# Layer two's second product as seven products of sums, its gates kept on the chip

## The chip, the cores and the metric

One core of a Trainium2 chip. The metric is the device time of one execution in microseconds, the median of several runs. The engines are TensorE (PE, matmuls, with its weight loads as PEld), VectorE (DVE), ScalarE (ACT), GpSimd (POOL, hardly used here) and SyncE (SP), whose queue issues nearly all transfers.

## The reference

An attention over small windows makes 3072 tokens of 512 numbers. Two layers follow, each a product to 2048 hidden numbers, a gate, and a product back to 512. All is float32.

```
x = attn_out.transpose(0, 2, 1, 3).reshape(3072, 512)
h = x @ w_in1;  g = s * relu(h)**2 + b;            x = g @ w_out1
h = x @ w_in2;  g = h * 1 / (1 + exp(-1.702 * h)); x = g @ w_out2
```

## The kernel before

**Precision.** A matmul operand is held as two pieces, a high part `h` and the rest `l`, and a product is three matmuls: high x high, high x rest, rest x high. "A split" is what makes the pieces: a cast (ACT, sometimes DVE) and a subtraction (DVE).

**Blocks.** The tokens form six blocks of 512. Attention and layer one of blocks 0 to 3 run first (`step`, one unit per block and hidden tile of 128, `j` from 0 to 15; the very first units are 256 tokens wide). Then four stages run, `SEVEN`: layer one of blocks 4 and 5 (stage 0), and layer two of blocks 0 and 1, 2 and 3, 4 and 5 (stages 1 to 3). A stage takes a pair of blocks, `bp` and `bq`, and is one call of `seven(s)`.

**First product of a stage.** Tokens, hidden numbers and the 512 inner numbers are each cut in halves, and the four quarter results are had from seven products of sums instead of eight (Winograd's form of Strassen's scheme). The sums of the weights (`S1` to `S4`) are made once and lie in memory (`wc`); the sums of the tokens (`T1` to `T4`) are made at the stage's start, out of the second layer's input `y1`. One step `p` (8 in a stage, two hidden tiles each) runs the products A, B, A2, C, D, C2, D2, six matmuls of 512 columns each, into the accumulators `ph` (A and C) and `pb` (B and D). Between them ACT copies A's first half (`p1`, L1081) and DVE makes five additions (L1083 to L1101) into four buffers `ys`, each 128 x 512. A2 waits for `p1`, C2 for the addition `u3`, D2 for the addition `c22` (L1094).

**Gates.** Each step gives four gates: two for `bp` (`gh`, `gl`) and two for `bq` (`gq`). In layer two a gate is a sigmoid (ACT, L997), a multiplication (DVE, L1006), a cast (ACT, L1019) and a subtraction (DVE, L1022). Those of `bp` are used in the next step. Those of `bq` go to memory (`gd`, L1041) and come back later (L1136, tiles `gh`, `gl` or `back`), apart from the last two.

**Second product.** `out_of` multiplies one gate by a tile of `w_out`: 12 matmuls of 512 columns (4 slices, 3 terms, L1059) into `accA` and `accB`. The 16 of `bp` run between the products of the steps, the 16 of `bq` after them as a second group. `w_out2` is prepared by `outer(j)`, stored in `wod`, and read back into the 16 tiles `wo` before stage 1 (`reload`); the tiles stay for all three stages.

**Order.** Every instruction group is an `op` with a due mark, durations, dependencies and buffers. A planner (`Plan.order`) plays all of them once and fixes each engine's order; at run time an engine works through its list and waits where its next instruction must. Buffers are counted by tag: `wi` (12 pairs of weight tiles, streamed in stages), `wz` (4), `u` (4), `st` (3), `h` (2, for `ph`), `a`, `accA`, `accB` and `ys` (1 each).

## Time and profile before

| | us |
|---|---|
| median of 3 runs (lowest, highest) | 1108.02 (1105.91, 1109.97) |
| the profiled execution's span | 1110.2 |
| PE busy in it | 1088.7 |
| DVE busy | 711.0 |
| ACT busy | 494.2 |
| attention and layer one of blocks 0 to 3 | to about 448 |
| stage 0 (layer one, blocks 4 and 5) | about 448 to 615 |
| stages 1, 2, 3 (layer two) | about 615 to 779, 779 to 943, 943 to 1106 |

A matmul's record lasts longer than its turn on the engine, since matmuls overlap; the distance of two starts is its price. The column PEclk is the granted clock of TensorE, 1.00 being full speed. "Idle" of an engine names what ended the wait.

### The profile page before, as it was taken

The page shows a single profiled execution, that of the slowest core. Times are in us where ns is not written, and L with a number is a line of the kernel's source. Part 1 is how long each engine was busy: PE and PEld are TensorE (multiplying, and loading weights), DVE is VectorE, ACT ScalarE, POOL GpSimd, SP SyncE. Part 2 cuts the span into 40 slices and gives each one's busy share as a digit, 9 for nine tenths or more (in the row PEclk, how much of TensorE's full clock was granted, in tenths as well). Part 3 has the DMA queues.
Part 4 walks back from the last instruction along what each step waited for, and adds up shares of the span by engine and source line. Part 5 has one row for each costly group of instructions (what it writes and reads, how often), then busy time and mean ns, then how long its engine had stood idle before and what let it go on. Part 6 is the DMA issues. An engine that isn't in the chain of part 4 may idle for free.

```text
span 1110.2 us, 20092 instructions
## 1 busy us (share of the span) xinstructions
PE 1088.7 (98%) x7852; PEld 897.8 (81%) x7852; DVE 711.0 (64%) x1241; ACT 494.2 (45%) x842; POOL 0.7 (0%) x6
## 2 busy tenths in 40 slices
PE   8879999999999999999999999999999999999998
PEld 7768887888878788888888888888888888888886
DVE  6888988878778688687881455660555760655610
ACT  4678865555445455566640433330433430333310
POOL 0000000000000000000000000000000000000000
PEclk9999999999999999999999999999999999999999
DMA  8776627756678783888999965574755574654154
GB/s 326 245 258 209 208 105 248 259 193 219 208 275 267 265 301 117 312 294 279 318 323 382 322 203 200 183 260 144 246 188 201 202 246 155 203 190 142 76 191 150
DMA packets 119406, 252.99 MB, mean 228 GB/s; under 512 B 12816, under 2 KB 29200, under 8 KB 119312
## 3 DMA queue, kind: packets, MB, share of 16 engines
q1 hardware_dynamic: 119024, 251.19, 66.1%
q8 instruction: 62, 1.02, 0.4%
q10 hardware_dynamic: 288, 0.52, 0.1%
q14 instruction: 32, 0.26, 0.1%
HBM read 169.87 MB, written 81.79 MB: 227 GB/s over the span
## 4 chain that ended last, share of the span: by engine, by line
PE 92%; DMA 3%; DVE 2%; issue 1%; ACT 1%; SPq 0%; ACTq 0%; DVEq 0%
PE accA L1059 16%; PE accB L1059 16%; PE accA L640 7%; PE accB L640 7%; PE ph L981 5%; PE ph L983 5%; PE ph L982 5%; PE ph L602 5%; PE ph L603 5%; PE ph L604 5%; PE pb L983 4%; PE pb L981 4%; PE pb L982 4%; DMA st<-w_in 2%; PE o L479 1%; PE sc L418 1%
## 5 line engine op out<-in xcount | busy, mean ns | idle before, releaser
L997 ACT ACTIVATE r<-ys 128x512 f32<-128x512 f32 x72 | 45.5, 632 | 107.6 <-DVE ys L1094 81.2
L1083 DVE TENSOR_TENSOR ys<-pb,ys 128x512 f32<-128x512 f32 x32 | 22.0, 686 | 91.6 <-DMA out<-y 58.7
L602 PE MATMUL ph<-xh,wih 128*128 128x512 f32 (+1 forms) x200 | 79.3, 396 | 0.6 <-DVE xh L223 0.6
L603 PE MATMUL ph<-xl,wih 128*128 128x512 f32 (+1 forms) x200 | 76.6, 383 | 0.7 <-DVE xl L510 0.7
L604 PE MATMUL ph<-xh,wil 128*128 128x512 f32 (+1 forms) x200 | 76.4, 382 | 0.0
L223 ACT COPY y<-accA 128x512 f32<-128x512 f32 x20 | 10.9, 590 | 138.5 <-issue 84.4
L609 ACT ACTIVATE r<-ph 128x512 f32<-128x512 f32 (+1 forms) x66 | 38.5, 584 | 60.4 <-PE ph L604 54.2
L624 ACT CAST gh<-r 128x512 fp32r<-128x512 f32 (+1 forms) x66 | 40.2, 609 | 47.8 <-PE accB L640 31.2
L1094 DVE TENSOR_TENSOR ys<-pb,ys 128x512 f32<-128x512 f32 x32 | 22.1, 691 | 53.9 <-PE pb L983 53.3
L1006 DVE TENSOR_TENSOR r<-ph,r 128x512 f32<-128x512 f32 x24 | 16.6, 691 | 62.2 <-ACT r L997 62.2
L1059 PE MATMUL accA<-woh,gh 128*128 128x512 f32 x138 | 54.0, 391 | 0.0
L1059 PE MATMUL accA<-woh,gl 128*128 128x512 f32 x138 | 53.9, 390 | 0.0
L1059 PE MATMUL accB<-woh,gh 128*128 128x512 f32 x138 | 53.7, 389 | 0.0
L1059 PE MATMUL accA<-wol,gh 128*128 128x512 f32 x138 | 53.7, 389 | 0.0
L1059 PE MATMUL accB<-woh,gl 128*128 128x512 f32 x138 | 53.7, 389 | 0.0
L1059 PE MATMUL accB<-wol,gh 128*128 128x512 f32 x138 | 53.7, 389 | 0.0
L640 PE MATMUL accA<-gl,woh 128*128 128x512 f32 (+1 forms) x132 | 50.9, 385 | 2.2 <-DVE gl L628 2.2
L1019 ACT CAST gh<-r 128x512 fp32r<-128x512 f32 x64 | 39.8, 622 | 29.1 <-DVE r L1006 21.7
L342 ACT ACTIVATE st<-st 128x512 f32<-128x512 uint32 x64 | 42.8, 676 | 22.4 <-DMA st<-w_out 10.7
L640 PE MATMUL accA<-gh,woh 128*128 128x512 f32 (+1 forms) x132 | 51.4, 389 | 1.3 <-ACT gh L624 1.3
L640 PE MATMUL accB<-gl,woh 128*128 128x512 f32 (+1 forms) x132 | 50.6, 383 | 1.2 <-issue 1.2
L640 PE MATMUL accB<-gh,woh 128*128 128x512 f32 (+1 forms) x132 | 51.0, 387 | 0.0
(210 smaller groups left out, 2973.6 us busy)
## 6 DMA issues: line engine op xcount, KB each, us to landing
gd<-gq SPq DMA_DIRECT2D x56, 512.0 KB, 2.7
wih<-wch SPq DMA_DIRECT2D x96, 256.0 KB, 3.5
wil<-wcl SPq DMA_DIRECT2D x96, 256.0 KB, 3.8
st<-w_in SPq DMA_DIRECT2D x32, 512.0 KB, 5.4
st<-w_out SPq DMA_DIRECT2D x32, 512.0 KB, 5.0
back<-gd SPq DMA_DIRECT2D x56, 256.0 KB, 3.1
k<-k_w SPq DMA_DIRECT2D x24, 512.0 KB, 5.6
v<-v_w SPq DMA_DIRECT2D x24, 512.0 KB, 6.1
```

The source lines that it names most:

```text
L342: nc.scalar.activation(out=lo.bitcast(F32), in_=lo, func=AF.Copy, scale=2.0**-51, bias=2.0)
L602: nc.tensor.matmul(ph, wh, xh, start=(k == 0), stop=False)
L603: nc.tensor.matmul(ph, wh, xl, start=False, stop=False)
L604: nc.tensor.matmul(ph, wl, xh, start=False, stop=(k == KT - 1))
L624: nc.scalar.copy(out=T["g", i][0], in_=T["r", i])
L640: nc.tensor.matmul(o, lt, rh, start=fresh and x == 0, stop=(done and x == 2))
L981: nc.tensor.matmul(ph, wh, xh, start=first and i == 0, stop=False, skip_group_check=True)
L982: nc.tensor.matmul(ph, wh, xl, start=False, stop=False, skip_group_check=True)
L983: nc.tensor.matmul(ph, wl, xh, start=False, stop=i == 1, skip_group_check=True)
L997: nc.scalar.activation(out=T[rk], in_=src(), func=AF.Sigmoid, scale=GATE)
L1019: nc.scalar.copy(out=T[key][0], in_=T[rk])
L1059: nc.tensor.matmul(a, lt, rh, start=n == 0 and x == 0, stop=n == NF - 1 and x == 2)
```

## The change

Stages 1 to 3 run a new function, `wino(s)`; stage 0 still runs `seven(0)`. In `wino`:

- The eight steps of the first product run without the second product between them, in the order A, B, C, A2, D, C2, D2. Steps with odd `p` use `accA` and `accB` (names `pc`, `pd`) in place of `ph` and `pb`.
- The gate is one activation (`Gelu_apprx_sigmoid`), written unsplit into one tile `G` that holds all 32 gates of the stage. It lies where the gates and `w_out` tiles of the earlier stages were. Nothing goes to `gd` and back.
- The second product has the same seven-product form. It runs after the first, product by product in the order 0, 4, 1, 5, 3, 6, 2. Each takes 16 gates' worth of `G` (8 tiles, or sums of them made in place), in four portions of two tiles: a cast and a subtraction on 1024 columns make the pieces, in a ring of three buffer pairs (`oj`, `oj`, `oq`). Each tile then takes 12 matmuls with 256 columns (4 slices of 128 tokens, 3 terms), with the gate's piece as the loaded operand.
- The four quarter results are put together by two pairs of ACT copies and six pairs of DVE additions, and each is stored as it is ready.
- `w_out2` is prepared in pairs (`outer(p)`), with its sums, into `wod`, and every stage streams it through the `wi` tiles. Four pairs are prepared up to stage 0, four not before the end of stage 0's first product. `wi` has 8 tiles in place of 12; four others (`wj`) serve as ring.
- The planner counts an operation that takes two buffers of one tag.

```
-NWI = 12
+NWI = 8
+NWJ = 4
+HELD = 4
...
+    plan.tag("wi", NWI)
+    plan.tag("wj", NWJ)
+    plan.tag("wo", NF)
+    plan.tag("wz", NF - NWI - NWJ)
+    plan.tag("q", 2)
...
+    def outer(p, late=()):
+
+        need = 10.0 * (len(units) + 10) + 1380
+        i0, i1 = [("two", 1, 2 * p + x) for x in range(2)]
+        a, b = [words(i, (1, 1, i[2]), need, late) for i in (i0, i1)]
...
+        def sums(e):
+            fresh(1)
+            fresh(2)
+            v0, v1 = u(i0), u(i1)
+            for x, y, z in ((raw(2)[:, hi], v0[:, hi], v0[:, lo]), (raw(1)[:, hi], v1[:, hi], v0[:, hi]),
+                            (raw(1)[:, lo], v1[:, hi], raw(2)[:, hi]), (raw(2)[:, lo], v1[:, lo], raw(1)[:, lo])):
+                nc.vector.tensor_tensor(out=x, in0=y, in1=z, op=ALU.subtract)
...
+        ku, kv = ("u", i0), ("u", i1)
+        done = parts_of(0, lambda: u(i1), 512, [b], [kv], slice(1, 3), True)
+        d = op(need, {"dve": 1.7}, sums, after=[a, b], alloc=[("st", ("qo", p, 1)), ("st", ("qo", p, 2))], uses=[ku, kv])
+        done += parts_of(1, lambda: raw(1), 512, [d], [], slice(3, 5), False)
+        done += parts_of(2, lambda: raw(2), 512, [d], [], slice(5, 7), False)
+        done += parts_of(3, lambda: u(i0)[:, lo], 256, [a], [ku], slice(0, 1), True)
+        o_wod[p] = done
...
+    def wino(s):
+        m, bp, bq = SEVEN[s]
+        base = 10.0 * (len(units) + 10) + 1000 * s
+        slot, holds, ready = operands(s)
+        o_in = {(p, n): stream(s, p, n, base + 40 * p - 0.5) for p in range(NF // 2) for n in range(4)}
...
+        def g_of(ty, z):
+            if not g_tile:
+                g_tile.append(pools["gg"].tile([P, 4, HALF, 512], F32, tag="G", name="G"))
+            return g_tile[0][:, ty, z]
...
+        def space(c, p):
+            if p % 2:
+                return ("accA" if c in "AC" else "accB", ("two", s, p, c in "AC"), "ABCD".index(c) // 2)
+            return ("h", ("h", s, p, c), None) if c in "AC" else ("a", ("two", s, p, False), "BD".index(c))
...
+        def gates(src, ty, p, need, d, uses):
+            def first(e):
+                nc.scalar.activation(out=g_of(ty, p), in_=src(), func=AF.Gelu_apprx_sigmoid if m else AF.Relu)
+
+            def square(e):
+                nc.scalar.activation(out=g_of(ty, p), in_=g_of(ty, p), func=AF.Square)
+
+            def affine(e):
+                nc.vector.tensor_scalar(out=g_of(ty, p), in0=g_of(ty, p), scalar1=sb[:, 0:1], scalar2=sb[:, 1:2], op0=ALU.mult, op1=ALU.add)
+
+            a = b = op(need, {"act": 0.62}, first, after=d + o_gp + free_g.get((ty, p // 2), []), uses=uses)
+            if not m:
+                b = op(need, {"act": 0.62}, square, after=[b])
+                b = op(need, {"dve": 0.54}, affine, after=[b])
+            o_g[ty, p] = b
+            return a
...
+            A = product(p, "A", "A11", "B11", at, [], True)
+            p1 = op(at + 4, {"act": 0.6}, lambda e, p=p, one=one: nc.scalar.copy(out=spot(one), in_=bank("A", p)),
+                    after=[A] + s_one.get(one, []), alloc=[("ys", tmp)] if p == 0 else [], uses=[tmp, space("A", p)[1]])
+            B_ = product(p, "B", "S2", "T2", at + 5, [], True)
+            u2 = add(one, "B", one, at + 9, [B_, p1])
+            C = product(p, "C", "S3", "T3", at + 10, [], True)
+            u3 = add(1, "C", one, at + 14, [C, u2] + s_22)
+            A2 = product(p, "A", "A12", "B21", at + 15, [A, p1], False)
+            D = product(p, "D", "S1", "T1", at + 20, [], True)
+            c22 = add(1, "D", 1, at + 24, [D, u3])
+            C2 = product(p, "C", "A22", "T4", at + 25, [C, u3], False)
+            c21 = add(2, "C", one, at + 29, [C2, u2] + s_21)
+            D2 = product(p, "D", "S4", "B22", at + 30, [D, c22], False)
+            c12 = add(one, "D", one, at + 34, [D2, c21, u3])
...
+            gates(lambda p=p: bank("A", p), 0, p, at + 60, [A2], [space("A", p)[1]])
...
+        at = base + 400
+        pairs_ = [slice(2 * x, 2 * x + 2) for x in range(HALF // 2)]
+        o_s3 = [op(at, {"dve": 1.22}, lambda e, z=z: nc.vector.tensor_tensor(
+            out=g_of(2, z), in0=g_of(0, z), in1=g_of(2, z), op=ALU.subtract),
+            after=[o_g[ty, 2 * x + i] for ty in (0, 2) for i in range(2)]) for x, z in enumerate(pairs_)]
...
+        SOURCE = {0: 0, 4: 2, 1: 1, 5: 3, 3: 2, 6: 0, 2: 1}
+        BANKS = {0: ("a", 0), 4: ("accA", 0), 1: ("accB", 0), 5: ("accA", 0), 3: ("a", 1), 6: ("accB", 1), 2: ("accA", 1)}
...
+            tag = "wj" if rung[0] % 3 else "q"
+            rung[0] += 1
...
+            def high(e):
+                for k in (kh, kl):
+                    T[k] = wp.tile([P, 2, 512], F32R, tag="wj", name="oj", bufs=NWJ) if tag == "wj" else pools["gg"].tile(
+                        [P, 2, 512], F32R, tag="q", name="oq", bufs=2)
+                nc.scalar.copy(out=T[kh], in_=g_of(ty, z))
+
+            def left(e):
+                nc.vector.tensor_tensor(out=T[kl], in0=g_of(ty, z), in1=T[kh].bitcast(F32), op=ALU.subtract)
+
+            h = op(need, {"act": 1.05}, high, after=o_raw[ty, x], alloc=[(tag, kh), (tag, kl)], uses=[kh])
+            l = op(need, {"dve": 1.22}, left, after=[h], uses=[kh, kl])
...
+                gh, gl = [T[key + (v,)][:, p % 2] for v in "hl"]
+                wh, wl = [w[:, p % 2 * 256:p % 2 * 256 + 256] for w in T["wp", s, n, p // 2]]
+                if m:
+                    for t in range(4):
+                        z = slice(t * P, t * P + P)
+                        a = acc[:, t // 2, t % 2 * 256:t % 2 * 256 + 256]
+                        for x, (lt, rh) in enumerate(((gh, wh), (gh, wl), (gl, wh))):
+                            nc.tensor.matmul(a, lt[:, z], rh, start=first and t % 2 == 0 and x == 0,
+                                             stop=p == HALF - 1 and x == 2, skip_group_check=True)
...
+        for i, n in enumerate((0, 4, 1, 5, 3, 6, 2)):
+            here = at + 70 * i
+            wait = [got["y7", b] for b in range(2)] if n == 5 else []
+            prev = []
+            for x in range(HALF // 2):
+                if n == 3:
+                    sums(x, 2, 3, 2, ALU.subtract, here + 16 * x, o_part[4, x])
+                elif n == 6:
+                    sums(x, 0, 0, 2, ALU.add, here + 16 * x, o_part[0, x])
+                elif n == 2:
+                    sums(x, 1, 1, 2, ALU.subtract, here + 16 * x, o_part[1, x])
+                key = split(n, x, here + 16 * x)
+                d = weights_of(n, x, here + 16 * x - 0.5)
+                for p in (2 * x, 2 * x + 1):
+                    prev = [outer_product(n, p, here + 8 * p, key, d, prev + wait)]
...
+                elif n == 3:
+                    got["u2", b] = evac(n, b, b, b, e, [got["y1", b], got["c11", b]])
+                    got["c21", b] = away(5, b, b, e, [got["u2", b]], True, True)
+                elif n == 6:
+                    got["u4", b] = evac(n, b, b, b, e, [got["u2", b], got["c21", b]])
+                    away(None, b, b, e, [got["u4", b], got["y7", b]], False, True)
+                elif n == 2:
+                    away(n, b, b, e, [got["u4", b]], False, False)
...
-        outer(2 * p)
-        outer(2 * p + 1)
-    for s in range(len(SEVEN)):
-        if s == 1:
-            for j in range(NF):
-                reload(j)
-        seven(s)
+    for p in range(HELD):
+        outer(p)
+    one = len(plan.ops)
+    seven(0)
+    two = len(plan.ops)
+    for p in range(HELD, NF // 2):
+        outer(p, step_end)
+    step_ops.extend(range(one, two))
+    o_gp = [op(-1, {"none": 0.0}, follow("gp", "gg", bufs=1), after=step_ops)]
+    for s in range(1, len(SEVEN)):
+        wino(s)
```

**Place 1: PE, the second product, before in stage 2, after at its start in stage 1.** Names: `woh`, `wol`, `wih`, `wil` are pieces of `w_out2`; `gh`, `gl`, `oq`, `oj` pieces of gates. Before:

```order
L1059 MATMUL accA_8126<-woh_7120,gh_8323 128x512
L1059 MATMUL accA_8126<-wol_7121,gh_8323 128x512
L1059 MATMUL accA_8126<-woh_7120,gl_8324 128x512
...
L1059 MATMUL accB_8143<-woh_7120,gh_8323 128x512
L1059 MATMUL accB_8143<-wol_7121,gh_8323 128x512
L1059 MATMUL accB_8143<-woh_7120,gl_8324 128x512
```

After:

```order
L1358 MATMUL pb_7786<-wih_7672,oq_7240 128x256 [waits DMAHW7_49,PE_49]
L1358 MATMUL pb_7786<-wil_7673,oq_7240 128x256 [waits DMAHW0_49]
L1358 MATMUL pb_7786<-wih_7672,oq_7241 128x256
...
L1358 MATMUL pb_7786<-wih_7691,oj_7416 128x256 [waits DMAHW1_49]
L1358 MATMUL pb_7786<-wil_7692,oj_7416 128x256 [waits DMAHW2_49]
L1358 MATMUL pb_7786<-wih_7691,oj_7417 128x256
```

Twelve wide matmuls a tile, into two accumulators, became twelve of half the width into one, with new pieces of weights and gates every 24.

**Place 2: DVE, a step of the first product at the start of stage 2.** `ys<-pb` and `ys<-ph` are the additions, in the order u2, u3, c22, c21, c12. Before, with the multiplications and subtractions of the gates (`r`, `gl`, `gq`) between:

```order
L1083 TENSOR_TENSOR ys<-pb,ys 128x512 [waits PE_49]
L1022 TENSOR_TENSOR gq<-r,gq 128x512 [waits Activation_49]
L1006 TENSOR_TENSOR r<-ph,r 128x512 [waits Activation_49]
L1087 TENSOR_TENSOR ys<-ph,ys 128x512 [waits DVE_49,PE_49]
L1022 TENSOR_TENSOR gl<-r,gh 128x512 [waits Activation_49]
L1094 TENSOR_TENSOR ys<-pb,ys 128x512 [waits DVE_49,PE_49]
L1097 TENSOR_TENSOR ys<-ph,ys 128x512 [waits PE_49]
L1006 TENSOR_TENSOR r<-ys,r 128x512 [waits DMAHW7_49,Activation_49]
L1101 TENSOR_TENSOR ys<-pb,ys 128x512 [waits DVE_49,PE_49]
```

After, an odd step (`pc`, `pd`) and the start of the next:

```order
L1273 TENSOR_TENSOR ys<-pd,ys 128x512 [waits PE_49,Activation_49]
L1273 TENSOR_TENSOR ys<-pc,ys 128x512 [waits DVE_49,PE_49]
L1273 TENSOR_TENSOR ys<-pd,ys 128x512 [waits DVE_49,PE_49]
L1332 TENSOR_TENSOR oq<-G,oq 128x1024 [waits Activation_49]
L1273 TENSOR_TENSOR ys<-pc,ys 128x512 [waits PE_49]
L1273 TENSOR_TENSOR ys<-pd,ys 128x512 [waits DVE_49,PE_49]
L1297 TENSOR_TENSOR G<-G 128x1024 [waits Activation_49]
L1273 TENSOR_TENSOR ys<-pb,ys 128x512 [waits PE_49,Activation_49]
```

After, in stage 1's second step, where the preparation of `w_out2` (`u`, `st`) is still going on:

```order
L1273 TENSOR_TENSOR ys<-pc,ys 128x512 [waits DVE_49,PE_49,Activation_49]
L358 TENSOR_SCALAR u<-u 128x512 [waits DVE_49]
L362 ISA u<-st,u 128x1024 [waits DVE_49,Activation_49] x2
L366 SCALAR_TENSOR_TENSOR u<-st,u 128x512 [waits DVE_49]
L1273 TENSOR_TENSOR ys<-pd,ys 128x512 [waits PE_49]
```

The gates' four operations are gone; in stage 2 one split (`oq<-G`) and one first sum (`G<-G`) stand behind the third and the fifth addition, in stage 1 four operations of the preparation between the second and the third.

**Place 3: DVE, the turn from the fifth to the sixth product of the second product, stage 1.** Before, in the second group, only the next stage's operands stand on DVE, ahead of that stage's first addition:

```order
L899 TENSOR_TENSOR xf<-xf,u 128x512
L223 CAST wzh<-xf 128x512 [waits DVE_49]
L914 TENSOR_TENSOR wzl<-xf,wzh 128x512 [waits DVE_49]
L914 TENSOR_TENSOR wzl<-xf,wzh 128x512 [waits Activation_49]
L1083 TENSOR_TENSOR ys<-pb,ys 128x512 [waits DMAHW3_49,DMAHW4_49,DMAHW0_49,DMAHW7_49,PE_49,Activation_49]
```

After:

```order
L1332 TENSOR_TENSOR oq<-G,oq 128x1024 [waits PE_49,Activation_49]
L1374 TENSOR_TENSOR ys<-pb,ys 128x512 [waits PE_49]
L1374 TENSOR_TENSOR ys<-pb,ys 128x512
L1384 TENSOR_TENSOR y<-pc,ys 128x512 [waits DVE_49]
L1384 TENSOR_TENSOR y<-pc,ys 128x512 [waits DMAHW7_49,DVE_49]
L1332 TENSOR_TENSOR oj<-G,oj 128x1024 [waits Activation_49]
```

Four additions out of the accumulators of the product that has just ended now stand between two splits; 22 of the stage's 28 splits are ahead of them, for 20 portions that PE has used by then.

## Rows read from the trace of the kernel before

**Rows 1.** The page's head and its first row of engines.

```profile
span 1110.2 us, 20092 instructions
PE 1088.7 (98%) x7852; PEld 897.8 (81%) x7852; DVE 711.0 (64%) x1241; ACT 494.2 (45%) x842; POOL 0.7 (0%) x6
```

**Rows 2.** Windows: length, busy us of each engine, granted clock, DMA share, GB/s.

```profile
448.00:569.00 121.00, 120.90 (x532) 99.30 (x531) 98.93 (x182) 76.88 (x136) 0.00 (x0) 1.00 0.87 305
569.00:615.00 46.00, 46.00 (x202) 37.80 (x203) 15.66 (x28) 5.79 (x11) 0.00 (x0) 1.00 1.00 360
...
779.00:943.00 164.00, 164.00 (x721) 134.98 (x720) 82.91 (x132) 51.73 (x88) 0.00 (x0) 1.00 0.61 205
```

**Rows 3.** Waits of PE from 448 to 1106 us: total us, times, longest.

```profile
PE ph L981 <- ACT ys L1081: 0.3, 1, 0.3
```

**Rows 4.** The chain that ended last: start us, us, what.

```profile
732.47 1.36 PE accB L1059 x6
733.83 1.47 PE accA L1059 x6
735.29 1.40 PE accB L1059 x6
...
897.93 1.47 PE accA L1059 x6
...
1062.03 1.47 PE accA L1059 x6
```

**Rows 5.** Timeline of PE, matmuls of 256 columns: start us, us, what.

```profile
35.35 0.28 PE L604 MATMUL ph<-xh,wil 128*128 128x256 f32 x1
...
36.41 0.28 PE L604 MATMUL ph<-xh,wil 128*128 128x256 f32 x1
36.53 0.28 PE L640 MATMUL accA<-gh,woh 128*128 128x256 f32 x1
...
37.85 0.28 PE L640 MATMUL accB<-gh,wol 128*128 128x256 f32 x1
37.97 0.28 PE L602 MATMUL ph<-xh,wih 128*128 128x256 f32 x1
```

**Rows 6.** Timeline of the weight loads in the same stretch.

```profile
36.42 0.19 PEld L640 LDWEIGHTS accA<-gh,woh 128*128 128x128 f32 x1
36.53 0.19 PEld L640 LDWEIGHTS accA<-gl,woh 128*128 128x128 f32 x1
...
37.86 0.19 PEld L602 LDWEIGHTS ph<-xh,wih 128*128 128x128 f32 x1
```

**Rows 7.** Groups by line and form: busy us, mean ns, idle before.

```profile
L1006 DVE TENSOR_TENSOR r<-ys,r 128x512 f32<-128x512 f32 x72 | 49.2, 683 | 0.0
...
L1022 DVE TENSOR_TENSOR gl<-r,gh 128x512 fp32r<-128x512 f32 x64 | 44.1, 690 | 2.4 <-ACT gh L1019 2.0
...
L755 DVE TENSOR_TENSOR st<-st 128x1024 fp32r<-128x1024 f32 x8 | 9.7, 1217 | 0.3 <-ACT st L751 0.3
...
L751 ACT CAST st<-st 128x1024 fp32r<-128x1024 f32 x8 | 8.4, 1050 | 0.3 <-DVE st L747 0.2
```

**Rows 8.** Timeline of a step of stage 2: D's end, the addition, D2's start.

```profile
799.14 0.39 PE L983 MATMUL pb<-xl,wil 128*128 128x512 f32 x1
...
799.57 0.69 DVE L1094 TENSOR_TENSOR ys<-pb,ys 128x512 f32<-128x512 f32 x1 [2.79 <-PE pb L983]
...
800.73 0.39 PE L981 MATMUL pb<-wzh,wih 128*128 128x512 f32 x1
```

**Rows 9.** Timeline of the end.

```profile
1105.42 0.39 PE L1059 MATMUL accB<-woh,back 128*128 128x512 f32 x1
1105.89 1.07 ACT L223 COPY y<-accB 128x512 f32<-128x512 f32 x2 [0.28 <-ACT y L223]
```

**Rows 10.** Transfers and an activation in the page's groups: count, KB, us to landing; busy, mean ns.

```profile
gd<-gq SPq DMA_DIRECT2D x56, 512.0 KB, 2.7
L997 ACT ACTIVATE r<-ys 128x512 f32<-128x512 f32 x72 | 45.5, 632 | 107.6 <-DVE ys L1094 81.2
```

More of the change, by code (lines that the diff above doesn't have):

```diff
@@ L211, in attention_moe_moe @@
     wc = [[[dram.tile([P, 7, 256], F32, name=f"wc{x}{m}{p}") for x in "hl"] for p in range(NF // 2)] for m in range(2)]
-    wod = [dram.tile([P, 2, 512], F32, name=f"wod{j}") for j in range(NF)]
+    wod = [[dram.tile([P, 7, 2, 256], F32, name=f"wod{x}{p}") for x in "hl"] for p in range(NF // 4)]
     gd = [dram.tile([P, 2, 512], F32, name=f"gd{j}") for j in range(NF)]
@@ L358, in words @@
         st, u = ("st", i), ("u", i)
-        a = op(need, {"sp": 1.55}, load, alloc=[("st", st)])
+        a = op(need, {"sp": 1.55}, load, after=late, alloc=[("st", st)])
         c = op(need, {"act": 0.67}, low, after=[a], uses=[st])
@@ L823, in attention_moe_moe @@
     o_wod = {}
-    def outer(j):
-        need = 10.0 * (len(units) + 10) + 920
-        i = ("two", 1, j)
-        a = words(i, (1, 1, j), need)
-        key = ("q", "o", j)
-        def high(e):
-            T[key] = stp.tile([P, 2, 512], F32R, tag="st", name="st")
-            copy(e, T[key][:, 0], T["u", i].bitcast(F32))
-        def left(e):
-            x = T[key]
-            nc.vector.tensor_tensor(out=x[:, 1], in0=T["u", i].bitcast(F32), in1=x[:, 0].bitcast(F32), op=ALU.subtract)
-        a = op(need, {"act": 0.62, "dve": 0.36}, high, after=[a], alloc=[("st", key)], uses=[("u", i)])
-        a = op(need, {"dve": 0.65}, left, after=[a], uses=[("u", i), key])
-        o_wod[j] = op(need, {"sp": 1.45}, lambda e: nc.sync.dma_start(out=wod[j], in_=T[key].bitcast(F32)), after=[a], uses=[key])
@@ L844, in reload, with u, fresh, raw @@
-    def reload(j):
-        w = (1, 1, j)
-        def fn(e):
-            T[w] = weight_tiles("wo")
-            for v in range(2):
-                nc.sync.dma_start(out=T[w][v].bitcast(F32), in_=wod[j][:, v])
-        need = 10.0 * (len(units) + 10) + 1000 + 30 * j
-        o_w[w] = [op(need, {"sp": 1.45}, fn, after=[o_wod[j]], alloc=[("wo", w)])]
-    def seven(s):
+    def outer(p, late=()):
+        need = 10.0 * (len(units) + 10) + 1380
+        i0, i1 = [("two", 1, 2 * p + x) for x in range(2)]
+        a, b = [words(i, (1, 1, i[2]), need, late) for i in (i0, i1)]
+        lo, hi = slice(0, 256), slice(256, 512)
+        def u(i):
+            return T["u", i].bitcast(F32)
+        def fresh(n):
+            T["qo", p, n] = stp.tile([P, 2, 512], F32R, tag="st", name="st")
+        def raw(n):
+            return T["qo", p, n][:, 1].bitcast(F32)
+        def sums(e):
[5 more added lines that the diff above has]
+                nc.vector.tensor_tensor(out=x, in0=y, in1=z, op=ALU.subtract)
+        def parts_of(n, src, w, after, key, cols, alloc):
+            def high(e):
+                if alloc:
+                    fresh(n)
+                copy(e, T["qo", p, n][:, 0, :w], src())
+            def left(e):
+                x = T["qo", p, n]
+                nc.vector.tensor_tensor(out=x[:, 1, :w], in0=src(), in1=x[:, 0, :w].bitcast(F32), op=ALU.subtract)
+            def store(v):
+                return lambda e: nc.sync.dma_start(
+                    out=wod[p // 2][v][:, cols, p % 2], in_=T["qo", p, n][:, v, :w].bitcast(F32).rearrange("p (n d) -> p n d", d=256))
+            f = w / 512
+            x = op(need, {"act": 0.12 + 0.5 * f, "dve": 0.4}, high, after=after, alloc=[("st", ("qo", p, n))] if alloc else [], uses=key)
+            y = op(need, {"dve": 0.15 + 0.54 * f}, left, after=[x], uses=key + [("qo", p, n)])
+            return [op(need, {"sp": 0.75 * f}, store(v), after=[z], uses=[("qo", p, n)]) for v, z in enumerate((x, y))]
+        ku, kv = ("u", i0), ("u", i1)
[5 more added lines that the diff above has]
+        o_wod[p] = done
@@ L1156, in attention_moe_moe @@
                     attend(u)
+        one = len(plan.ops)
         step(i)
+        step_ops.extend(range(one, len(plan.ops)))
     for u in parts:
```

192 lines of the change are left out of this document (170 added, 22 removed).

## The prediction

> **What bounds the kernel now.** I read the page's engine row first: TensorE (PE) is busy for 1088.7 of 1110.2 us [rows 1]. The reader is to see that this leaves 21.5 us of idling, and that a saving can only come from PE having less to do. Busy time of pipelined matmuls proves little by itself, so the second view is the list of what PE waited for in layer two (448 to 1106 us): one wait of 0.3 us in 658 us [rows 3]. So PE sets the pace there, at full clock (1.00 in the windows) [rows 2], which is the 2.4 GHz level. Third, the pace itself: in the chain that ended last, six matmuls of 512 columns take 1.36 us in most rows, 0.2267 us each; in a few they take 1.40 to 1.47 us [rows 4]. The start of the second group of the second product recurs at 733.83, 897.93 and 1062.03 us [rows 4]: a stage of layer two lasts 164.10 us. It has 336 matmuls in the first product (8 steps x 7 products x 6) and 384 in the second (2 groups x 16 x 12): 720 x 0.2267 = 163.2 us. The 0.9 us left are the slow rows, 1.2 ns a matmul on average.
>
> **The matmuls of the second product (stages 1 to 3).** The change replaces 384 matmuls of 512 columns by 7 products x 8 steps x 12 = 672 of 256 columns. By columns that is 7/8; by the clock it is not, because a matmul has a price beside its columns. The trace has this shape, in layer one's first units: twelve of 256 columns from 36.53 to 37.97 us, 0.1200 us each, and nine from 35.35 to 36.41 us, 0.1178 us each [rows 5]. Each carries its own weight load; the loads start 0.12 us apart and last 0.19 us, so they overlap one another and the matmuls [rows 6]. I take 0.1200, the one of the twelve whose operands are a gate's pieces and a second weight, as here. New stage: 336 x 0.2267 + 672 x 0.1200 = 76.2 + 80.6 = 156.8 us, and the slow rows scaled by the number of matmuls (0.9 x 1008/720 = 1.3): 158.1 us. That is 6.0 us less a stage, **18.1 us** for three.
> Bounds: at 0.1178 a stage gains 7.4 us, in all 22.3. At the other end, the extra of the slow rows could lie on every narrow matmul: 1.40 us for six is 6.7 ns more each, 0.1267 us, which leaves 1.6 us a stage, some 5 in all; 1.47 for six is 18 ns more, 0.138 us, a loss of 6.0 us a stage, 18 in all. Averaged over a stage the extra was 1.2 ns, so I stay near the first end, and keep 0.1267 for the range.
> The Trainium skill speaks against the change here: "TensorE: Matmul & The Clock Gate", in "LDWEIGHTS (loading the stationary operand)", puts a load of 128 columns at 128/1.2 ns, and in "The mechanism" lets a load overlap a running matmul only where their row groups differ. Every load here uses all rows; so, as an estimate by that page, a narrow matmul would take 107 + 107 = 213 ns and a wide one 320, a stage's second product 143.4 in place of 122.9 us, and the change would cost 62 us. This trace does not agree: 120 and 227 ns, loads included. The same page's gap without loads ("Back-to-back issue gap": columns/2.4 plus 2.5 ns) gives 215.8 and 109.2 ns, an estimate of 28 us gained; the trace's extra is some 13 ns a matmul, not 2.5, and that difference is what twice as many matmuls pay.
>
> **VectorE, and the buffers it fills.** Per stage the change takes away the 32 multiplications by the sigmoid (L1006, 683 ns) and 32 subtractions (L1022, 690 ns) [rows 7], and the 28 stores and reads of gates through memory (gd, 56 issues in the whole kernel, of which 14 should stay) [rows 10]. It adds 28 splits, 12 sums and 4 first sums on 1024 columns (1217 ns [rows 7], a form of the weight preparation) and 12 additions out of the accumulators (691 ns, L1094 [rows 8]). VectorE in a stage: 40 additions of the first product 27.6, splits 34.1, sums 19.5, additions 8.3, the next stage's operands some 17: 106 us, against 82.9 before [rows 2]. Still below 158. ScalarE gets 28 casts of 1050 ns, loses 32 of 512 columns, and keeps 32 gates, whose single activation I price like the sigmoid, 632 ns [rows 10]; at twice that it would have 20 us more of over 100 that it idles in a stage [rows 2]. Both lie beside PE's work as long as they come in time, and three places decide that.
> First, inside a step of the first product, now packed into 9.5 us with nothing of the second product between. The tightest hand-over is the addition between product D and its second half D2, with only product C2 (1.36 us) as cover. It was as tight before: the last matmul of D starts at 799.14, the addition runs from 799.57 for 0.69 us, and D2 starts at 800.73 [rows 8], 0.47 us after the addition's end. In stages 2 and 3 VectorE's list has nothing ahead of that addition (place 2 of the order above). In stage 1 four operations of w_out2's preparation stand there in its second step (place 2), some 2.5 us between the additions u3 and c22, whose products end 2.7 us apart: I allow **1.0 us** of PE waits in this stage, between 0 and 0.5 us for each of its eight steps (4 us).
> Second, the ring of the second product: three pairs of split gates, each used for 24 matmuls, 2.88 us. When one is used up, the next but two is cast (1.05) and split (1.22), 2.3 us, while two others last 5.76. Slack 3.4 us.
> Third, the turn from the fifth product to the sixth and from the sixth to the seventh: there four additions (2.8 us) stand ahead of the split (place 3): 2.8 + 1.2 = 4.0 of 5.76 us. Slack 1.7 us. In the second product VectorE is busy for 25 splits 30.4, sums 14.6, additions 8.3 and most of the operands 13: 66 of 82 us. I take no PE wait in second and third place, and keep them as a rival.
>
> **The rest.** Transfers: a stage reads 28 x 512 KB of w_out2's pieces where it wrote 14 and read 14 x 512 KB of gates: the same. The last part of stage 0 (569 to 615 us) kept the DMA engines busy at a share of 1.00, while PE did not idle [rows 2]; half of w_out2's preparation and its 16 reloads leave it. With PE fully busy there is nothing to gain; I take 0, between 0 and -0.5. On SP, the issue queue, a load waits for its buffer and an output store for its addition; both wait for the same matmuls at most, and loads run 8 buffers, over 20 us, ahead. The gates' tile lies where layer one's weights and gates were, so the first gate of stage 1 waits for stage 0's last matmul; products of the next step stand behind it on PE, so 0. The table load of the activation is there once before and once after.
> The end: now PE's last matmul starts at 1105.42, ScalarE copies twice in 1.07 us, and the span ends 4.4 us after PE [rows 1, 9]. After, both halves of the last accumulator are ready together, and VectorE adds twice (1.38 us): **+0.4 us**, between 0 and 1.
> Sum, against the profiled execution: 1110.2 - 18.1 + 1.0 + 0.4 = 1093.5 us. Its span is 2.2 us over the median of the runs (1108.02; 1105.91 to 1109.97), so from the median: 1108.0 - 16.7 = **1091 us**.
>
> **The rivals.** (a) VectorE becomes the bound of the second product. For it: 66 of 82 us busy, and two turns with 1.7 us of slack. Against it: from 448 to 569 us it was busy for 99 of 121 us [rows 2] without holding PE. It decides from VectorE arriving 1.7 us late at a turn; late by 2 to 4 us at six turns and a little between costs 5 to 15 us: 1097 to 1106, say 1100.
> (b) The narrow matmul at 0.1267 us: 1108.0 - 4.9 + 1.4, 1104 to 1105. For it: that pace appears for whole rows [rows 4], and more loads in the same time mean more reads. Against it: the mean of a stage.
> (c) Slower: the loads do not stay hidden when hundreds of narrow matmuls follow one another, where the trace has a streak of 36. It decides from 0.129 us a matmul (the second product's 87.0 us now, less 0.4 us for more slow rows, over 672). If each had to wait out its own load, 0.19 us [rows 6], a stage would grow by 672 x 0.188 - 87.0 = 39 us: 1227 us in all. Against it: the loads of [rows 6] overlap without a gap. This is also where the page's rule above would lead.
> (d) The gain is larger, at 0.1178 us and without waits: 1086.
>
> **How the numbers follow.** Forecast (1086 to 1097) 0.76; (a) 0.10, half of it below 1104.7; (b) 0.06, about half there; (c) 0.06; better than 1085 0.02. A measurement of this kernel tells some 0.3% (3.3 us) from no change. Faster by more than that: 0.76 + 0.02 + 0.06 + 0.03 = 0.87; within: 0.07; slower: 0.06. The range goes from 1085 to 1102, from (d) to past the middle of (a), and leaves out (c), most of (b) and the far ends.
>
> **What would show it.** Right: in the second product of stages 1 to 3 narrow matmuls 0.118 to 0.122 us apart, stages of some 158 us, PE waits of under 1 us in stages 2 and 3 and some 1 us in stage 1, VectorE some 106 us a stage, 14 stores of gates in all. Wrong, by (a): PE waits for VectorE's split in the second product. By (b) or (c): no waits, but wider spacing of the narrow matmuls. By the first place: PE waits for VectorE's addition at the second half of D.

## The result and the profile after

The changed kernel takes **1094.15 us** (median of 4 runs, 1091.54 to 1096.69), the kernel before in the same session 1108.99 (4 runs, 1105.91 to 1112.23): a ratio of 0.9869, with a 95% interval from 0.9842 to 0.9897. The forecast was 1091, the range 1085 to 1102. The profiled execution spans 1094.8 us; its own forecast, 1110.2 of [rows 1] with the same terms, was 1093.5. As a gain, 16.7 us were forecast; between the two profiled executions it was 15.4, between these medians 14.8. The 1091 started from a median of 1108.0 (3 runs), which became 1109.0 with the fourth run.

The page's head, its row of engines, and the groups that answer to [rows 7] and [rows 10] (busy us, mean ns, idle before and what ended it):

```profile
span 1094.8 us, 21993 instructions
PE 1074.3 (98%) x8716; PEld 924.5 (84%) x8716; DVE 780.8 (71%) x1259; ACT 529.3 (48%) x840; POOL 0.7 (0%) x6
...
L1329 ACT CAST oj<-G 128x1024 fp32r<-128x1024 f32 x54 | 56.7, 1050 | 75.9 <-PE pd L1358 30.1
L1332 DVE TENSOR_TENSOR oj<-G,oj 128x1024 fp32r<-128x1024 f32 x54 | 66.0, 1222 | 23.5 <-ACT oj L1329 23.4
...
L1251 ACT ACTIVATE G<-ys 128x512 f32<-128x512 f32 x72 | 45.4, 631 | 48.4 <-DVE ys L1273 48.4
```

The stores of gates, in the list of transfers (count, KB, us to landing):

```profile
gd<-gq SPq DMA_DIRECT2D x14, 512.0 KB, 4.0
```

PE is busy for 14.4 us less with 864 matmuls more, VectorE for 70 us more. The 14 stores of gates left are stage 0's, as forecast. The new splits cost what the weight preparation's operations of that shape did, and the single activation (L1251, 631 ns) what the sigmoid did.

The windows of stages 1 to 3, cut at the borders of the two products (length, then busy us of PE, weight loads, VectorE, ScalarE and GpSimd, granted clock, DMA share, GB/s); they answer to [rows 2]:

```profile
616.10:691.50 75.40, 74.69 (x321) 59.43 (x320) 52.98 (x89) 36.50 (x61) 0.00 (x0) 1.00 0.86 284
691.50:772.10 80.60, 80.60 (x674) 80.60 (x672) 61.13 (x66) 33.91 (x40) 0.00 (x0) 1.00 0.74 228
772.10:850.50 78.40, 78.20 (x338) 62.68 (x337) 38.81 (x54) 28.65 (x46) 0.00 (x0) 1.00 0.62 196
850.50:931.10 80.60, 80.60 (x673) 80.56 (x673) 61.20 (x66) 33.98 (x40) 0.00 (x0) 1.00 0.65 203
931.10:1009.20 78.10, 78.01 (x338) 62.84 (x338) 35.36 (x47) 26.63 (x42) 0.00 (x0) 1.00 0.62 194
1009.20:1089.80 80.60, 80.60 (x673) 80.58 (x671) 52.06 (x49) 29.05 (x31) 0.00 (x0) 1.00 0.52 164
```

The chain of what ended last, at the start of stage 3's second product and at the end (start us, us, what); it answers to [rows 4] and [rows 9]:

```profile
1009.36 11.51 PE pb L1358 x96
...
1078.47 11.53 PE pc L1358 x96
1090.01 0.03 issue
1090.03 0.69 DVE y L1384
```

Each of the 21 products of the three second products (seven a stage) stands in the chain as one piece of 96 matmuls and 11.51 to 11.53 us: 0.1200 us a matmul, without a wait, a second product of 80.6 us. The start of the second product recurs after 159.1 and 158.7 us; 158.1 was forecast, 164.1 it was. The list of waits of PE from 440 to 1092 us has one row for stages 1 to 3 ([rows 3]; total us, times, longest):

```profile
PE pd L1240 <- DVE ys L1273: 0.5, 1, 0.5
```

But the first products, 336 matmuls at 0.2267 = 76.2 us, take 78.4 and 78.0 in stages 2 and 3, from the first start to the next product's. That time is found only by taking the starts of PE's matmuls and looking for distances over 0.29 us. In the first products of stages 1 to 3 there are fifteen places, each two distances long. **Twelve are alike**: one in each odd step, before the second half of product C, of 0.41 to 0.47 and then 0.33 or 0.34 us, 0.30 us more than two normal distances (0.36 in stage 1's second step); 3.7 us together. Three stand before D's second half: 0.73 us more in stage 1's second step, 0.40 in the last step of stages 1 and 2; 1.5 us together. All of them: **5.2 us**. The waits view misses nearly all of it, since a matmul's modelled length (0.39 us) covers a gap of 0.41.

The timeline of an odd step of stage 2, PE, VectorE and ScalarE (start us, us, engine, line, operation, tiles; in brackets the idle time before and what ended it):

```profile
806.47 0.39 PE L1242 MATMUL pc<-xs,wil 128*128 128x512 f32 x1
806.90 0.69 DVE L1273 TENSOR_TENSOR ys<-pc,ys 128x512 f32<-128x512 f32 x1 [1.99 <-PE pc L1242]
807.62 0.60 ACT L1251 ACTIVATE G<-pc 128x512 f32<-128x512 f32 x1 [4.19 <-DVE ys L1273]
807.86 0.40 PE L1242 MATMUL pd<-xl,wil 128*128 128x512 f32 x1
808.27 0.19 PEld L1240 LDWEIGHTS pc<-wzh,wih 128*128 128x128 f32 x1 [0.45 <-ACT G L1251]
808.27 0.50 PE L1240 MATMUL pc<-wzh,wih 128*128 128x512 f32 x1
...
808.61 0.39 PE L1241 MATMUL pc<-wzl,wih 128*128 128x512 f32 x1
```

In odd steps A and C are the two halves of one accumulator tile, `pc`, and waits are kept for whole tiles. The addition u3 needs only C, which ended at about 805.5; it starts at 806.90, when A's second half is through. A's gate starts when u3 is, and C's second half starts when the gate has read the tile, at 808.27. Four steps that need not follow one another do so.

The last step of stage 2 has another reason; the same view:

```profile
846.50 0.68 DVE L946 TENSOR_TENSOR xh<-xf,xh 128x512 fp32r<-128x512 f32 x1
847.10 1.29 DVE L931 TENSOR_TENSOR xf<-xf 128x512 f32<-128x512 f32 x2
...
848.31 0.68 DVE L1273 TENSOR_TENSOR ys<-pd,ys 128x512 f32<-128x512 f32 x1
848.54 0.40 PE L1242 MATMUL pc<-wzh,wil 128*128 128x512 f32 x1
...
849.05 0.51 PE L1240 MATMUL pd<-wzh,wih 128*128 128x512 f32 x1
```

The addition c22 (848.31) has the next stage's operands (L946, L931) ahead of it on VectorE, and D's second half waits for c22.

### The profile page after: what moved, and what is told of

Read it like the earlier page. It is cut to its first block, busy times and chain, and to the rows that moved or that the text cites. A ratio compares the mean times of both kernels' runs of the same rounds, so it can differ in the third digit from the quotient of the medians.

```text
span 1094.8 us, 21993 instructions
## 1 busy us (share of the span) xinstructions
PE 1074.3 (98%) x8716; PEld 924.5 (84%) x8716; DVE 780.8 (71%) x1259; ACT 529.3 (48%) x840; POOL 0.7 (0%) x6
## 4 chain that ended last, share of the span: by engine, by line
PE 91%; DMA 3%; DVE 3%; issue 1%; ACT 1%; DVEq 0%; SPq 0%; ACTq 0%
PE pc L1358 9%; PE accA L652 7%; PE accB L652 7%; PE pd L1358 6%; PE pb L1358 6%; PE ph L614 5%; PE ph L615 5%; PE ph L616 5%; PE accA L1098 4%; PE accB L1098 4%; PE pc L1240 2%; PE ph L1240 2%; PE ph L1242 2%; PE ph L1241 2%; PE pc L1242 2%; PE pc L1241 2%
## 5 line engine op out<-in xcount | busy, mean ns | idle before, releaser
L1329 ACT CAST oj<-G 128x1024 fp32r<-128x1024 f32 x54 | 56.7, 1050 | 75.9 <-PE pd L1358 30.1
L1332 DVE TENSOR_TENSOR oj<-G,oj 128x1024 fp32r<-128x1024 f32 x54 | 66.0, 1222 | 23.5 <-ACT oj L1329 23.4
L1251 ACT ACTIVATE G<-ys 128x512 f32<-128x512 f32 x72 | 45.4, 631 | 48.4 <-DVE ys L1273 48.4
L1358 PE MATMUL pc<-wih,oj 128*128 128x256 f32 x336 | 62.4, 283 | 0.0
L640 DVE TENSOR_TENSOR gl<-r,gh 128x512 fp32r<-128x512 f32 (+1 forms) x66 | 44.1, 669 | 14.4 <-ACT gh L636 14.0
L1358 PE MATMUL pd<-wih,oj 128*128 128x256 f32 x288 | 53.8, 283 | 0.0
L1358 PEld LDWEIGHTS pc<-wih,oj 128*128 128x128 f32 x336 | 53.3, 192 | 0.0
L1332 DVE TENSOR_TENSOR oq<-G,oq 128x1024 fp32r<-128x1024 f32 x30 | 36.7, 1224 | 20.6 <-ACT oq L1329 20.6
L652 PE MATMUL accA<-gh,wol 128*128 128x512 f32 (+1 forms) x132 | 50.8, 385 | 0.0
L652 PE MATMUL accB<-gh,wol 128*128 128x512 f32 (+1 forms) x132 | 50.5, 383 | 0.0
```

Of the source, the lines that this page charges most:

```text
L640: nc.vector.tensor_tensor(out=gl, in0=T["r", i], in1=gh.bitcast(F32), op=ALU.subtract)
L652: nc.tensor.matmul(o, lt, rh, start=fresh and x == 0, stop=(done and x == 2))
L1251: nc.scalar.activation(out=g_of(ty, p), in_=src(), func=AF.Gelu_apprx_sigmoid if m else AF.Relu)
L1329: nc.scalar.copy(out=T[kh], in_=g_of(ty, z))
L1332: nc.vector.tensor_tensor(out=T[kl], in0=g_of(ty, z), in1=T[kh].bitcast(F32), op=ALU.subtract)
L1358: nc.tensor.matmul(a, lt[:, z], rh, start=first and t % 2 == 0 and x == 0, stop=p == HALF - 1 and x == 2, skip_group_check=True)
```

## The experiments

The times of the kernels below stand against the changed kernel, which was run again beside two groups of them: 1093.6 us (4 runs) and 1096.21 us (4 runs); with the first four, 12 runs, the median is 1095.2. One execution of a kernel differs from another by some 5 us, much of it ahead of stage 1 (stage 0's last matmul started at 616.1, 613.3 and 615.5 us in the three traces of the changed kernel, whose spans were 1094.8, 1092.1 and 1094.2), so single steps are read from the trace: from the start of stage 0's last matmul (L1098) to that of the last of all took 473.6, 473.7 and 473.7 us in these three.

> The changed kernel once more, beside the three that follow, so that they are compared on one chip. Expected: 1094 us, with twelve pauses of TensorE of 0.3 us (four in each of stages 1 to 3, at product C's second half in the odd steps) and three at D's second half (1.5 us together), all in the first products, and 0.1200 us a matmul in the second products.

The twelve and the three places were there again, each distance within 0.02 us of the first trace's, and the second products took the same 80.6 us.

**The gate behind C's second half.**

```diff
-            gates(lambda p=p: bank("A", p), 0, p, at + 60, [A2], [space("A", p)[1]])
+            gates(lambda p=p: bank("A", p), 0, p, at + 60, [A2] + ([C2] if p % 2 else []), [space("A", p)[1]])
```

> In the odd steps of the first product the gate of A is ordered behind the second half of C, nothing else. A and C are two halves of one accumulator tile there. Theory 1 (the gate of A holds the tile, and C's second half waits for it): all twelve pauses before C's second half go, 12 x 0.30 = 3.6 us, 1090.5 us. Rival (the pause is the addition u3, which itself has to wait for A's second half because of the shared tile, or the accumulator's own turn): the pauses stay, 1094 us. Second rival: the gate, now 1.4 us later, delays the additions or the first split of the second product, and the 3.6 us come back there.

1092.96 us (4 runs); 471.6 us, 2.1 less. In the timeline of an odd step C's second half now follows D without a gap, though u3 still starts behind A's second half:

```profile
805.97 0.69 DVE L1273 TENSOR_TENSOR ys<-pc,ys 128x512 f32<-128x512 f32 x1 [1.99 <-PE pc L1242]
806.46 0.40 PE L1240 MATMUL pd<-xl,wih 128*128 128x512 f32 x1
807.15 0.40 PE L1240 MATMUL pc<-wzh,wih 128*128 128x512 f32 x1
...
809.46 0.60 ACT L1251 ACTIVATE G<-pc 128x512 f32<-128x512 f32 x1 [0.75 <-DVE ys L1273]
```

All twelve pauses are gone, so it was the gate and not u3. But 2.1 us came of 3.7: the pauses at D's second half grew. The distance of the two starts there went in the last step of stages 1 and 2 from 0.51 to 0.81 us, in stage 1's second step from 0.85 to 1.20, and a new one of 0.74 came in its sixth. PE's pause had been cover for c22; where c22 was late anyway, the time went from one place to the other. The second rival had the time come back, but not in this way.

**The next stage's operands behind c22, too.**

```diff
-            b11 = parts_of(i, "B11", [xs_[i]])
+            b11 = parts_of(i, "B11", [xs_[i]] + last_22)
...
-            b21 = parts_of(i, "B21", [xs_[i]])
+            b21 = parts_of(i, "B21", [xs_[i]] + last_22)
...
-        at = base + 400
+        at, last_22[:] = base + 400, [c22]
```

> As the run before, and VectorE's and ScalarE's operations for the next stage's operands start only behind the addition c22 of the last step of the first product. They then lie in the second product. Theory 1 (the pauses at D's second half in the last step of stages 1 and 2 come from the next stage's operands ahead of c22 on VectorE): two pauses of 0.4 us go, 1089.7 us; VectorE has room for the moved operations in the second product, where it was busy for 61 of 80.6 us. Rival: some 9 us more of VectorE's work in the second product makes the splits late, and TensorE waits there: 1092 us or more.

1092.05 us (5 runs); 470.2 us, 1.4 less again. No pause is left in the last steps. The second products stay at 80.6 us with the moved work in them:

```profile
689.70:770.30 80.60, 80.60 (x673) 80.58 (x672) 64.84 (x73) 34.77 (x41) 0.00 (x0) 1.00 0.70 229
```

VectorE does 64.8 us there in place of 61.1, and nobody waits. Two pauses are left, both in stage 1 (distances of 1.20 and 0.74 us). At the second, in the sixth step, VectorE has one subtraction of w_out2's preparation (L869) and a first sum of gates (L1297) ahead of c22; at the first its timeline has the preparation alone:

```profile
627.39 1.29 DVE L362 CUSTOM_DVE_ANT_0 u<-st,u 128x1024 uint16<-128x1024 uint16 x2
...
628.60 0.69 DVE L366 SCALAR_TENSOR_TENSOR u<-st,u 128x512 uint32<-128x512 uint32 x1
629.20 0.69 DVE L1273 TENSOR_TENSOR ys<-pd,ys 128x512 f32<-128x512 f32 x1
...
629.94 0.50 PE L1240 MATMUL pd<-wzh,wih 128*128 128x512 f32 x1 [0.81 <-DVE ys L1273]
```

**Without that preparation.**

```diff
-        outer(p, step_end)
+        o_wod[p] = o_wod[p - HELD]
...
-                    nc.sync.dma_start(out=T[key][v].bitcast(F32).rearrange("p (n d) -> p n d", d=256), in_=wod[x][v][:, n])
+                    nc.sync.dma_start(out=T[key][v].bitcast(F32).rearrange("p (n d) -> p n d", d=256), in_=wod[x % 2][v][:, n])
```

> As the run e7, and the half of w_out2's preparation that lies behind stage 0 is left out: the second half of the second product's weights is read from the first half's place. Theory (w_out2's preparation on VectorE, ahead of c22, is what is left of the pauses in stage 1): the two pauses at D's second half there, 1.6 us together, go, and no pause is left in the first products of stages 1 to 3: 1090.4 us, with everything else as it was. Rival (stage 1's pauses come from its transfers or from the overlap with stage 0): they stay.

1089.89 us (4 runs). Both pauses are gone, and stages 1 to 3 have no distance over 0.29 us on PE. Stage 1's first product takes 76.8 us, as those of stages 2 and 3 do. The planner's order changed too: none of stage 1's matmuls stands ahead of stage 0's last one here, where 18 do (4.1 us) in the changed kernel and in the run before (e7). So the 472.5 us behind that matmul don't compare with 470.2, and the run by itself doesn't tell the preparation from the overlap with stage 0. The timeline does: at both pauses the preparation stands ahead of c22, at the second with the first sum between them.

**A's second half behind C's.** With the causes known, one number removes them all: between D and D's second half there are two products then, and A's gate comes late by itself.

```diff
-            A2 = product(p, "A", "A12", "B21", at + 15, [A, p1], False)
+            A2 = product(p, "A", "A12", "B21", at + (27 if p % 2 else 15), [A, p1], False)
```

> The changed kernel with one number altered: in the odd steps A's second half comes after C's second half instead of before D. The addition u3 then doesn't have to wait for A's second half, A's gate comes behind C's second half by itself, and the addition c22 has two products (2.7 us) as cover in place of one (1.36). Theory (all pauses of the first products come from the one shared tile and from c22's short cover): the twelve pauses of 0.3 us and the three at D's second half go, 5.1 us of layer two, from stage 0's last matmul to the last one 468.6 us in place of 473.7; 1089 us. Rival (u3's cover, now D alone, 1.36 us, is too short in its turn, or c21, which now waits for A's second half, makes D's sum late): new pauses before C's second half or the next step, 1092 us or more.

The odd step's timeline in stage 2:

```profile
802.18 0.69 DVE L1273 TENSOR_TENSOR ys<-pc,ys 128x512 f32<-128x512 f32 x1 [0.60 <-PE pc L1242]
802.66 0.39 PE L1240 MATMUL pd<-xl,wih 128*128 128x512 f32 x1
803.34 0.39 PE L1240 MATMUL pc<-wzh,wih 128*128 128x512 f32 x1
803.54 0.69 DVE L1273 TENSOR_TENSOR ys<-pd,ys 128x512 f32<-128x512 f32 x1 [0.67 <-PE pd L1242]
...
806.09 0.40 PE L1240 MATMUL pd<-wzh,wih 128*128 128x512 f32 x1
```

c22 ends at 804.23 and D's second half starts at 806.09. None of the fifteen places is left; 468.4 us, 5.3 less (468.6 was expected). The median was 1091.54 (4 runs), only 2.1 below the changed kernel's of the session before, so both were timed on one chip:

> The changed kernel a third time, beside the next run on one chip, since the two were timed apart before. Expected: 1094 us and 473.7 us from stage 0's last matmul to the last of all.

> The kernel of e8_a2_behind_c2 once more, beside the changed kernel. Its trace had 5.3 us less between stage 0's last matmul and the end, its median was 2 to 3 us lower. If the trace is the whole difference: 5.3 us less than the run beside it (1089 us). If something in layer one takes back a part with the other order: 2 to 3 us less, with the stretch up to stage 0's last matmul longer.

1096.21 against **1088.55 us** (4 runs each), 7.7 less, where 5.3 were expected. In the two profiled executions 5.3 us of the difference lie behind stage 0's last matmul and 4.2 ahead of it (it started at 615.5 and 611.2 us). The second part isn't the edit's, since this kernel's first trace had 615.5 there, too. Over all runs it is 1095.2 (12) against 1089.7 (8), 5.5 less. Of the versions here that leave nothing out it is the fastest: 0.9813 of the kernel before, interval 0.9797 to 0.9828.

**What a narrow matmul costs.** With the gates as the moving operand (the other branch of `outer_product`) the second product has half as many matmuls, of 512 columns:

```diff
-                if m:
+                if not m:
                     for t in range(4):
```

> The second product of stages 1 to 3 with the weights as the stationary and 512 columns of gates as the moving operand: 336 matmuls of 512 columns in place of 672 of 256. What comes out is the transposed block (the stores write it as it lies), everything else is as in the changed kernel. By the spacing seen (0.2267 and 0.1200 us): 672 x 0.1200 - 336 x 0.2267 = 4.5 us less a stage, 13.4 us in all, 1080.7 us. Rival (a matmul costs its columns and the 13 ns are something of the narrow shape's surroundings, such as the first rows after a wait): no change, 1094 us. If VectorE is nearly the bound, the gain is under 13.4 us, with waits for the splits: it would have 76.2 us for the same work.

1081.32 us (4 runs); from stage 0's last matmul to the end 460.2 us, 13.5 less (13.4 expected). The chain has each product as

```profile
856.39 10.88 PE pc L1364 x48
```

which is 0.2267 us a matmul. The same columns in half as many matmuls save 0.64 us of 11.52. No wait for a split came up: VectorE's work of 60.5 us fitted into a second product of 76.2. The next run went the other way, to 128 columns:

```diff
-                            nc.tensor.matmul(a, lt[:, z], rh, start=first and t % 2 == 0 and x == 0,
+                            c = 128 if p else 256
+                            nc.tensor.matmul(a[:, :c], lt[:, z], rh[:, :c], start=first and t % 2 == 0 and x == 0,
                                              stop=p == HALF - 1 and x == 2, skip_group_check=True)
```

> The changed kernel with 588 of the 672 matmuls of each second product reading 128 columns in place of 256 (those of the first step keep 256; half of each block is then missing). Two questions. What a narrow matmul costs: by the columns and 13 ns, 53 + 13 = 67 ns; rival: the weight load behind it sets the pace and it stays at 120 ns, 1094 us and no waits. And where VectorE becomes the bound: at 67 ns TensorE needs 84 x 0.1200 + 588 x 0.067 = 49 us for a second product, VectorE was busy for 61 us in it; so TensorE would wait for the splits, and the second product would last some 61 to 66 us, 45 to 58 us less in all for the three stages: 1036 to 1049 us. With the cast and the subtraction one behind the other in three buffers it could be longer: 28 pairs x (1.05 + 1.22) / 2 = 32 us is no bound, so VectorE's list is.

1077.52 us (2 runs), some 18 less and not 45 to 58; 458.9 us from stage 0's last matmul to the end, 14.8 less. A product in the chain (twelve matmuls of 256 columns and 84 of 128), and two weight loads of it in the timeline, each with a matmul of 128 columns:

```profile
863.75 10.82 PE pd L1359 x96
```

```profile
865.07 0.19 PEld L1359 LDWEIGHTS pd<-wil,oj 128*128 128x128 f32 x1
865.18 0.19 PEld L1359 LDWEIGHTS pd<-wih,oj 128*128 128x128 f32 x1
```

A product takes 10.82 us: 12 x 0.1200 + 84 x 0.1117. So a matmul of a quarter of the wide one's columns costs 0.1117 us where 0.067 was expected, with PE never waiting: neither theory's number, but the rival's mechanism. The starts of the loads have the same distance, 0.11 us. That the load sets the pace there, and not the matmul itself, is seen where a product passes from its twelve wide matmuls to the narrow ones; the first three with 128 columns:

```profile
689.25 0.22 PE L1359 MATMUL pb<-wih,oq 128*128 128x128 f32 x1
689.31 0.28 PE L1359 MATMUL pb<-wil,oq 128*128 128x128 f32 x1
689.43 0.27 PE L1359 MATMUL pb<-wih,oq 128*128 128x128 f32 x1
```

In each of the 21 products the first two start 0.06 us apart, near the 0.067 expected. A load starts 0.12 us ahead of its matmul among the wide ones and 0.06 ahead from here on; with that lead spent, the matmuls keep the loads' 0.11 us. A fixed price of each pair of load and matmul isn't the reason either: in attention, pairs with a load of 32 columns start 0.01 us apart (median; L479 of the kernel before). The 256 columns of the change run 8 ns above that floor. The Trainium skill ("TensorE: Matmul & The Clock Gate", "LDWEIGHTS (loading the stationary operand)") puts a load of 128 columns at 128/1.2 = 107 ns; as the pace of loads in a row this trace agrees (111.7), while as a time added to each matmul, the estimate that the prediction worked out from the page, [rows 5] and the 0.1200 us of this kernel don't. Where VectorE becomes the bound this run didn't tell, since PE never became short enough.

**VectorE's room.** Every second split was made to subtract twice.

```diff
+                for _ in range(1 + x % 2):
                     nc.vector.tensor_tensor(out=T[kl], in0=g_of(ty, z), in1=T[kh].bitcast(F32), op=ALU.subtract)
```

> The changed kernel with the subtraction of every second split done twice: 14 x 1.22 = 17 us more for VectorE in each stage's second product, where it was busy for 61 of 80.6 us, so 78 of 80.6. Theory (three pairs of split gates cover a late split; VectorE isn't yet the bound): 0 to 4 us slower, 1094 to 1098, a few waits for the splits behind the turns with four additions. Rival (VectorE is at the edge already): TensorE waits at each doubled split, 0.5 us and more for each of 42: over 1110 us.

1105.17 us (10 runs), 10 us more than the changed kernel, where 0 to 4 were expected. Windows of the second products of stages 2 and 3, and the waits of PE:

```profile
856.60:941.70 85.10, 82.37 (x673) 80.96 (x672) 75.97 (x79) 33.89 (x40) 0.00 (x0) 1.00 0.62 191
1019.80:1102.00 82.20, 81.13 (x673) 80.68 (x672) 67.12 (x63) 29.11 (x31) 0.00 (x0) 1.00 0.50 160
```

```profile
PE pd L1359 <- DVE oj L1333: 2.2, 5, 0.8
PE pb L1359 <- DVE oj L1333: 2.1, 2, 1.1
```

The second products grew by 4.5 us in stages 1 and 2 and by 1.1 in stage 3, which has no next stage's operands to make. The longest pause, in stage 1:

```profile
741.75 1.05 ACT L1329 CAST oj<-G 128x1024 fp32r<-128x1024 f32 x1
742.32 1.89 DVE L946 TENSOR_TENSOR wzl<-xf,wzh 128x512 fp32r<-128x512 f32 x3
744.13 2.48 DVE L1333 TENSOR_TENSOR oj<-G,oj 128x1024 fp32r<-128x1024 f32 x2
...
746.66 0.51 PE L1359 MATMUL pb<-wih,oj 128*128 128x256 f32 x2 [1.07 <-DVE oj L1333]
```

The split's cast was done at 742.80, in time; its subtractions (744.13) stood behind three operations for the next stage's operands. Sorted by VectorE's busy time in a second product: 52.1, 61.1 and 64.8 us (the changed kernel's stages 3 and 1, and the run with the operands behind c22) cost PE nothing, 67.1 costs 1.1 us, 76.0 costs 4.5. So VectorE isn't the bound of the change, but some 4 to 6 us of work from it, as far as work in these places tells, and not the 19.5 us that it idles in stage 1's second product.

**The gate alone, in the kernel before.**

```diff
-                    nc.scalar.activation(out=T[rk], in_=src(), func=AF.Sigmoid, scale=GATE)
+                    nc.scalar.activation(out=T[rk], in_=src(), func=AF.Gelu_apprx_sigmoid)
...
-                    nc.vector.tensor_tensor(out=T[rk], in0=src(), in1=T[rk], op=ALU.mult)
+                    pass
```

> The kernel before with one part of the change alone: in stages 1 to 3 the gate is one activation, and the 96 multiplications on VectorE (683 ns each, 65.6 us) are gone. Theory (TensorE is the bound, VectorE's relief is worth nothing): within 0.3% of before, VectorE busy some 65 us less, the activation 0.63 us as the sigmoid. Rival (VectorE's share of the time lets through some of its relief): up to some us faster.

1109.61 us (12 runs) against 1108.84 (23 runs): a ratio of 1.0014, interval 1.0001 to 1.0027. The page's row of engines:

```profile
PE 1091.9 (98%) x7852; PEld 900.3 (81%) x7852; DVE 650.4 (58%) x1145; ACT 492.0 (44%) x842; POOL 0.7 (0%) x6
```

61 us less of VectorE (some 65 were expected) are worth nothing in a kernel that PE bounds. In the changed kernel they are part of the room that the 28 splits a stage need.

## Why the prediction came out right, step by step

- **The narrow matmuls: right to the digit.** 0.1200 us was read from a streak of twelve [rows 5], and 2016 of them ran at it; the second product is 80.6 us as summed. Rivals (b), (c) and (d), at 0.1267, from 0.129 and at 0.1178, are out. Only the likeness of the operands spoke for 0.1200 rather than 0.1178; what made the nine of [rows 5] faster stays open. That the loads were hidden was right at 256 columns, with less to spare than [rows 6] let see.
- **The slow rows: too much.** 1.3 us a stage had been scaled up by the number of matmuls. The second products have none; the first products, without their pauses, take 76.8 us (78.4 less 1.6, and as many in the run with A's second half behind C's), 0.6 over 76.2. That is some 2 us too much over three stages.
- **The first product: the failed step.** The prediction allowed 1.0 us of waits in stage 1 and none in stages 2 and 3, because "VectorE's list has nothing ahead of that addition". Measured: 2.4, 1.6 and 1.2 us. It had looked at one hand-over, D to D's second half, which was tight before too [rows 8], and at the order of one engine in one step. It missed that odd steps put A and C into one tile, so that C's second half waits for ScalarE's gate (3.7 us), and that the last step has the next stage's operands ahead of c22 (0.8 us). The term that it did have, w_out2's preparation, is 0.7 us.
- **VectorE in the second product (rival a): no wait**, as forecast; 61 us there where 66 were counted, since some of the operands are made in the first product (64.8 us in the run that moved them). Its stages take 114, 100 and 87 us, where some 106 were forecast for each. The slack of 1.7 us at the turns was never used up in the changed kernel; the doubled splits showed that the room is small.
- **The end: 0.3 us** (from the last matmul's start 5.1 us to the end of the span, 4.8 before), 0.4 forecast.
- The sum: 1093.5 + 4.2 for the first products - 2.1 for the slow rows is 1095.6, and 1094.8 was measured; what is left, under 1 us, lies ahead of stage 1 and was not taken apart. Two errors of opposite sign had partly cancelled: that the profiled execution came within 1.3 us of its forecast is in part luck.
- Two sums of the prediction are slightly off, and neither moves the forecast: 3 x (143.4 - 122.9) is 61 us and not 62, and the chance of a gain counts 0.06 of rival (a) where half of its 0.10 was said to lie below 1104.7.

## What to carry to other kernels

Price a matmul by a streak of its own shape in the trace, with the same loads, and trust it: columns over the clock would have said 0.107 us for 256 columns and 0.053 for 128, where 0.1200 and 0.1117 were measured. When accumulators of several products share a tile, every reader of one half holds the writers of the other, as the gate of A did here: order the second visit to a half behind the tile's other readers, or give it two products of cover, and look for the loss in the distances between starts, since the list of waits doesn't show gaps shorter than a modelled matmul. An idle share of another engine is no room by itself: what counts is what stands ahead of the one operation that is waited for.

## What the runs showed of the hardware

A stream of matmuls, each with its own load of 128 stationary columns, runs at 0.2267 us for 512 columns, 0.1200 for 256 and 0.1117 for 128, at a granted clock of 1.00: the first two are columns/2.4 GHz plus 13 ns, the third is the pace of the loads. The record of a load lasts 0.19 us in each case, so the records overlap one another, and their distance, not their length, is the price. I had expected 67 ns for 128 columns. The kernel before would have told: its attention has matmuls of that shape, each with its own load (L493), and the eight that start from 393.00 us on are 0.11 us apart.
